# A fused memory attention and two expert layers on one core: attention units seven rounds apart, second-layer weight conversions from block 18 on, three raw buffers, first weights loaded ahead, and the split of g issued later

## The chip, the cores and the metric

The kernel runs as one program on one core of a Trainium2 chip. The metric is the device time of one execution in microseconds (us); the number for the kernel before is the median of three runs.

## The reference

Three stages, all in float32; the weights of the two layers come as float64.

```python
a = softmax(phi, axis=sequence)                     # per batch, head: (576, 32)
k_m, v_m = a.T @ k, a.T @ v                         # (32, 64) each
attn = softmax(q @ k_m.T / sqrt(64), axis=-1) @ v_m
x = attn.transpose(0, 2, 1, 3).reshape(4608, 512)
h = x @ moe_w_in;   g = h - tanh(h);  x = g @ moe_w_out       # d_ff = 2048
h = x @ moe2_w_in;  g = where(h > 0, h, exp(min(h, 0)) - 1);  out = g @ moe2_w_out
```

There are 8 batches, 8 heads, 576 positions and 64 features a head; the layers see 4608 tokens of 512 features.

## The kernel before, in words

Every product is made of three matmuls on split operands: a float32 value is held as a rounded high part and the remainder (low part), and high·high, high·low and low·high are added in PSUM.

**Attention** (`Attention.unit`, lines 108 to 221) works in 16 units of four heads. A unit is a Python generator: each `yield` ends a round, and a unit lasts some 20 rounds. It reduces and exponentiates phi, makes k_m and v_m on TensorE (PE; `km`, line 147), transposes q (`pq`, line 171), forms scores (`sc`, line 192), a softmax over 32 slots, and writes the split probabilities p to memory (line 219). Units 0 and 1 run first; the start rounds of the units are given with `units.at`, for unit 4 and up round 19 and every 6th after.

**First layer** (`Moe1`). The output product of attention is folded into the first weight: `vw_half` (line 293) multiplies v_m by the converted w_in, so h is p times vw (`h_unit`, line 310). The loop over `blocks` (64 of them, index `bi`: two halves of d_ff, four groups of two batches, two sub-sweeps, four blocks of 288 tokens) does in each block two **steps**, i = 0 and 1, for two groups of 256 columns of d_ff. A step issues 12 matmuls of h (line 318), the activation (g_a on ScalarE (ACT), lines 329 to 332; g_b on GpSimd (POOL) and VectorE (DVE), lines 337 and 338; g_c, lines 343 and 344), the split of the g of the step before (g_d: the high part on ACT, line 350, the low part on POOL, line 351), and two x units of 12 matmuls (line 363) that multiply an earlier g by w_out. x units wait in the queue `xq`, so that an x unit uses a g that is about a block old. x goes to memory (line 378), and p of the next block is loaded a block ahead into two buffers (line 290). I number the steps 0 to 127 (step = 2·bi + i); each has one VectorE subtraction of line 338. In the last block of a group the next vw is made in both steps ("vw steps").

**Second layer** (`Moe2`): 18 blocks of 256 tokens, 8 steps each, from about 960 us to the end.

**Conversion of the weights** (`convert`, line 40, driven by `conv`, line 511). One conversion loads 512 KB of float64 words into a raw buffer (line 517 for w_in, 520 for w_out), and builds a float32 value from the two halves of each word: an absolute value into PSUM on ACT (line 48), four passes on DVE (lines 50, 51, 54, 55), the high part on ACT (line 58), the remainder on POOL (line 60). First-layer weights stay in SBUF; second-layer ones are written to memory (line 539) and loaded again in layer two. There are 32 conversions a layer.

What sets the order is a `Staged` queue for the units and one for the conversions (`cv`): a call of `round()` advances every live generator by one stage and starts the next one every `every` rounds. A step calls `cv.round()` once (twice in some blocks) and `units.round()` twice. Where something is not ready, a loop calls rounds on the spot: `need` for a converted weight, the loop on `p_done` for the p of the next block, and `cv.drain()` in `open_l2` at block 60, which opens the buffers of layer two. Each engine executes its instructions in the order in which this program issues them; all loads and stores are issued by SyncE (SP) in that order too.

Of the kernel before, what the change touches and what calls it, by code (L numbers as in the profile page):

```python
# [8 lines left out]
F32 = mybir.dt.float32  # L9
# [9 lines left out]
B, H, S, D, M = 8, 8, 576, 64, 32  # L19
# [16 lines left out]
def r32(ap):  # L36
    return ap.bitcast(F32)
# [25 lines left out]
class Attention:  # L63
# [5 lines left out]
    def __init__(self, tc, ctx, const, ins, vm, p_dram, side, psum):  # L69
        nc = tc.nc  # L70
        self.nc, self.ins, self.vm, self.p_dram = nc, ins, vm, p_dram
        self.ident, self.pmask, self.ones = const["ident"], const["pmask"], const["ones"]
        pool = lambda name, n: ctx.enter_context(
            tc.tile_pool(name=name + side, bufs=n, side=side, reuse_waits="tile"))
        self.wk = pool("at_wk", 1)
        self.sm = pool("at_sm", 3)
        self.sc_p = pool("at_sc", 2 if side == "left" else 1)
        self.ps = psum
        self.q_p = pool("at_q", 2)
        self.loaded = {}  # L80
        fix = pool("at_fix", 1)
        self.kv = fix.tile([128, 2, 4, 6, D], F32, name="kv")
        self.a = fix.tile([128, 6, 4, M], F32, name="a")
        self.kT = fix.tile([128, 4, 2, M], F32, name="kT")
        self.asum = fix.tile([128, 4, M], F32, name="asum")
        for t in (self.a, self.asum, self.kv):
            nc.gpsimd.memset(t[96:], 0.0)
        nc.gpsimd.memset(self.kT, 0.0)
# [19 lines left out]
    def unit(self, u, nxt, eng, first_p=None):  # L108

        nc, wk, sm = self.nc, self.wk, self.sm  # L110
        b, g = divmod(u, 2)
# [3 lines left out]
        ps_tile = lambda shape, name: self.ps.tile(shape, F32, tag="m", name=name)  # L115

        ph = self.loaded.pop((u, "phi"))
        cmax = wk.tile([96, 4, M], F32, tag="cmax", name="cmax")
        nc.vector.tensor_reduce(cmax, ph.rearrange("p h c m -> p h m c"), axis=AX.X, op=ALU.max)
        yield  # L120
        mT = ps_tile([128, 96], "mT")
        nc.tensor.transpose(mT, cmax.rearrange("p h m -> p (h m)"), ident[:96, :96])
        nmax = sm.tile([128, 1], F32, tag="nmax", name="nmax")
        nc.vector.tensor_reduce(nmax, mT, axis=AX.X, op=ALU.max)
        dmax = wk.tile([128, 128], F32, tag="dmax", name="dmax")
        nc.vector.tensor_scalar(dmax, ident, nmax, None, op0=ALU.mult)
        yield
        bmax = ps_tile([96, 4, M], "bmax")
        nc.tensor.matmul(bmax, lhsT=self.ones[:, :96], rhs=dmax, start=True, stop=True)
        bm = wk.tile([96, 4, M], F32, tag="cmax", name="bm")  # L130
        nc.scalar.activation(bm, bmax, ACTF.Copy)
        eng.tensor_tensor(ph, ph, bm.rearrange("p h (o m) -> p h o m", o=1).to_broadcast([96, 4, 6, M]),
                          op=ALU.subtract)
# [344 lines left out]
def moe_kernel(tc, q, k, v, phi, w1, w2, w3, w4, out):  # L478
    nc = tc.nc
    with ExitStack() as top, tc.manual_schedule():  # L480
# [9 lines left out]
        new = lambda stack, name, n, **kw: stack.enter_context(tc.tile_pool(name=name, bufs=n, reuse_waits="tile", **kw))  # L490
        l1a, l1b, l1c, at0_ctx, at1_ctx, wt_ctx, late_ctx, pro, ps_h_ctx = (ExitStack() for _ in range(9))
        m1 = Moe1(tc, l1a, const, p_dram, x2_dram)
        wt_p = {0: new(l1b, "wt0", 1, side="right")}
        vm_p = new(l1b, "vm", 2, side="right")
        cv_p = new(l1b, "cv", 3, side="right")
        raw_p = new(l1b, "raw", 2, side="right")
        wst_p = []
        misc = m1.misc = new(top, "ps_m", 3, space=PSUM)
        cv_ps = new(top, "ps_c", 1, space=PSUM)
# [7 lines left out]
        def need(kind, pg):  # L507
            while not all((1, kind, pg, c) in converted for c in range(2)):
                cv.round()

        def conv(layer, kind, pg, c):

            w = {("i", 1): w1, ("o", 1): w2, ("i", 2): w3, ("o", 2): w4}[kind, layer]
            raw = raw_p.tile([128, 512], mybir.dt.int64, tag="raw", name="raw")
            if kind == "i":
                src = w.rearrange("(k p) f -> p k f", p=128)[:, 2 * c:2 * c + 2, 256 * pg:256 * pg + 256]
                nc.sync.dma_start(out=raw.rearrange("p (a f) -> p a f", a=2), in_=src)
            else:
                r0 = 256 * pg + 128 * c
                nc.sync.dma_start(out=raw, in_=w[r0:r0 + 128, :])  # L520
            yield
            staged = []

            def dst():
                if layer == 1:
                    ws = wi if kind == "i" else wo
                    if c == 0:
                        pool = wt_p[pg // 2 % (2 if kind == "i" else NSW)]
                        shape = [128, 2, 4, 256] if kind == "i" else [128, 2, 2, 512]
                        ws[pg] = pool.tile(shape, F32R, tag=f"w{kind}{pg % 2}", name="w1")  # L530
                    return part(ws[pg], 0, c), part(ws[pg], 1, c)
                staged.append(wst_p[0].tile([128, 2, 512], F32R, tag="wst", name="wst"))
                return staged[-1][:, 0], staged[-1][:, 1]

            yield from convert(nc, cv_p, cv_ps, raw, dst)
            converted.add((layer, kind, pg, c))
            if layer == 2:
                yield
                nc.sync.dma_start(out=w_dram[kind][pg, :, :, 512 * c:512 * c + 512], in_=r32(staged[-1]))

        conv_pair = lambda layer, kind, pg: [conv(layer, kind, pg, c) for c in range(2)]
        conv_l1 = lambda kind, *pgs: [g for pg in pgs for g in conv_pair(1, kind, pg)]
        conv_l2 = [g for pg in range(NPG) for kind in "io" for g in conv_pair(2, kind, pg)]
# [7 lines left out]
        at0.p_done = at1.p_done = p_done = set()  # L551
        new_vm(0)
        nc.vector.memset(r32(vm[0]), 0.0)
        cv = Staged(conv_l1("i", 0, 1) + conv_l1("o", 0, 1), 2)
        for what in "phi", "kv", "q0", "q1":
            at0.load(0, what)
            at1.load(1, what)
        cv.round()

        def unit(u):  # L560
            if u % 4 == 0 and u:
                new_vm(u // 4)
            if u in (0, 2):
                yield from at0.unit(u, 2 if u == 0 else 2 * B, nc.vector if u == 0 else nc.gpsimd,
                                    first_p if u == 0 else None)
            else:
                yield from at1.unit(u, 3 if u == 1 else u + 1, nc.vector if u < 2 else nc.gpsimd,
                                    first_p if u == 1 else None)

        first_p = [m1.new_p(0, n) for n in range(2)]  # L570
        units = Staged()
        for u, t in ((0, 0), (1, 1), (2, 8), (3, 9)):
            units.at(t, unit(u))
        for u in range(4, 2 * B):
            units.at(19 + 6 * (u - 4), unit(u))
        while 1 not in p_done:
            units.round()
            if units.rounds >= 9:
                cv.round()
        pro.close()  # L580
        m1.ps_h = new(ps_h_ctx, "ps_h", 2, space=PSUM)
# [16 lines left out]
        LAG = 4  # L598
        xq, pend, late = deque(), [], []
        at0_open = at1_open = True  # L600

        def x_next(on_act):
            if len(xq) >= LAG:
                sw, n, dm = xq.popleft()
                for i in range(2):
                    need("o", 2 * sw + i)
                m1.x_unit(sw, n, dm, wo, on_act)
                if dm % 2 == 1:
                    late.append((sw, n, dm // 2))

        def store_late():
            while late:
                m1.store_x(*late.pop(0))
# [51 lines left out]
        for bi, (ss, bp, sub, j) in enumerate(blocks):  # L665
# [28 lines left out]
            if at1_open and 2 * B - 1 in p_done:  # L694
# [1 line left out]
                at1_open = False  # L696
                wt_p[3], wt_p[2] = new(l1c, "wt3", 1), new(late_ctx, "wt2", 1)
                cv.first.extend(conv_l1("o", 4, 5))
            if bi == 7:
                cv.todo.extend(conv_l2)  # L700
                cv.every = 3
            if bi == 24:
                cv.first.extend(conv_l1("i", 4, 5))
            if bi == 28:
                cv.first.extend(conv_l1("i", 6, 7) + conv_l1("o", 6, 7))
            if bi == 20:
                cv.every = 2
            if ss == 1 and j == 1 and sub == 1 and bp + 1 < B // 2 or bi == 29:
                load_vm((bp + 1) % (B // 2))
            if nxt and nxt not in m1.p:  # L710
# [1 line left out]
            for i in range(2):  # L712
                pg = 2 * sw + i
                m1.h_unit(sw, n, pg)
                m1.g_a(n, pg)
                m1.g_b(n, pg)
                if pend:
                    m1.g_d(*pend.pop())
                store_late()
                if soon:  # L720
                    soon.popleft()()
                x_next(True)
                cv.round()
                units.round()
                if vw_next:
                    vbp, vpg, pars = vw_next
                    need("i", vpg + i)
                    while ss == 0 and not all(u in vm_done for u in range(4 * vbp + 4)):
                        units.round()
                    m1.vw_half(vm[vbp], wi[vpg + i], vpg + i, 0, pars)  # L730
                if soon and bi > 60:
                    soon.popleft()()
                x_next(bi < 22)
                m1.g_c(n, pg)
                if bi < 7 or 28 <= bi < 30:
                    cv.round()
                units.round()
                if vw_next:
                    m1.vw_half(vm[vbp], wi[vpg + i], vpg + i, 1, pars)
                pend.append((n, pg))  # L740
# [6 lines left out]
        LAG = 1  # L747
# [50 lines left out]
```

## Time and profile before

| | |
|---|---|
| median of three runs | 1791.59 us (1788.22 to 1793.15) |
| the profiled execution | 1789.79 us |
| its span | 1787.6 us |
| PE busy in the span | 1613.6 us (90%) |
| DVE, ACT, POOL busy | 1255.0 (70%), 959.1 (54%), 763.8 us (43%) |
| bytes moved | 238.40 MB, 133 GB/s over the span |
| chain that ended last | PE 62%, DVE 13%, DMA 12%, ACT 6% |

The busy shares are means over stages that differ: attention and the first layer run together until about 490 us, the first layer alone until about 960 us, then the second layer. So the profile is read by stages.

### The profile page before, as it was taken

How to read it: one execution, taken by the hardware profiler on the slowest of the kernel's cores; microseconds unless marked ns; L12 is line 12 of the kernel's file. 1: busy time of each engine (PE TensorE's matmuls, PEld its weight loads, DVE VectorE, ACT ScalarE, POOL GpSimd, SP SyncE). 2: the span in 40 equal slices, each digit the busy share in tenths (PEclk: the TensorE clock that was granted, in tenths of full speed). 3: DMA queues.
4: the chain of work that ended last, by engine and by line, in shares of the span. 5: the costliest groups of instructions: out<-in, count | busy, mean ns of one | idle time of the engine just before them, and what ended most of it. 6: DMA issues, size and time to landing. Idle time of an engine off the chain costs nothing.

```text
span 1787.6 us, 30091 instructions
## 1 busy us (share of the span) xinstructions
PE 1613.6 (90%) x11496; PEld 1483.2 (83%) x11496; DVE 1255.0 (70%) x1805; ACT 959.1 (54%) x1713; POOL 763.8 (43%) x539
## 2 busy tenths in 40 slices
PE   4547787888898999898999999999999999999998
PEld 2336777778897999898999999999999999999997
DVE  5859887988788998888875555555555555555554
ACT  2436776777887887787875333333333333333332
POOL 2235655656665665566653222222222222222222
PEclk9758999999999999999999999999999999999999
DMA  9547577675455445555557621111121121211210
GB/s 214 165 118 191 157 204 215 198 224 181 170 167 168 153 168 190 205 198 205 188 189 276 249 61 57 59 59 58 55 62 58 59 59 57 60 57 59 60 36 24
DMA packets 140934, 238.40 MB, mean 133 GB/s; under 512 B 8184, under 2 KB 102392, under 8 KB 138744
## 3 DMA queue, kind: packets, MB, share of 16 engines
q1 hardware_dynamic: 140792, 236.49, 42.5%
q8 instruction: 91, 1.49, 0.4%
q14 instruction: 51, 0.42, 0.1%
HBM read 159.78 MB, written 75.50 MB: 132 GB/s over the span
## 4 chain that ended last, share of the span: by engine, by line
PE 62%; DVE 13%; DMA 12%; ACT 6%; issue 5%; POOL 2%; SPq 1%; DVEq 0%; ACTq 0%; POOLq 0%
PE h_ps L419 23%; PE o_ps L456 22%; PE x_ps L363 9%; PE h_ps L318 5%; DMA p<-p_dram 5%; DMA raw<-in_moe_w_in_dram 2%; DVE s L343 2%; DVE vw L308 2%; DMA q<-in_q_dram 1%; DMA raw<-in_moe_w_out_dram 1%; DVE h_ps L338 1%; DMA x_dram<-x 1%; ACT t L329 1%; PE vw_ps L303 1%; POOL g L351 1%
## 5 line engine op out<-in xcount | busy, mean ns | idle before, releaser
L363 PE MATMUL x_ps<-g,w 128*128 128x288 f32 x3072 | 448.7, 299 | 40.3 <-DVE vw L308 16.7
L363 PEld LDWEIGHTS x_ps<-g,w 128*128 128x128 f32 x3072 | 422.3, 190 | 52.1 <-ACT x L370 14.7
L419 PEld LDWEIGHTS h_ps<-x,wi 128*128 128x128 f32 x3456 | 429.7, 190 | 11.7
L445 POOL TENSOR_TENSOR e<-hm,e 128x512 fp32r<-128x512 f32 x144 | 186.5, 1295 | 587.3 <-ACT e L444 443.3
L419 PE MATMUL h_ps<-x,wi 128*128 128x256 f32 x3456 | 433.2, 281 | 0.0
L456 PE MATMUL o_ps<-wo,e 128*128 128x512 f32 x1728 | 423.8, 394 | 0.7 <-POOL e L445 0.7
L456 PEld LDWEIGHTS o_ps<-wo,e 128*128 128x128 f32 x1728 | 314.8, 188 | 65.0 <-POOL e L445 1.1
L430 ACT ACTIVATE t_ps<-hm 128x512 f32<-128x512 f32 x144 | 86.7, 602 | 514.3 <-DVE hm L429 514.3
L337 POOL TENSOR_TENSOR v<-t,u 128x576 f32<-128x576 f32 x128 | 183.2, 1431 | 269.2 <-ACT u L330 221.6
L318 PE MATMUL h_ps<-p,vw 128*128 128x288 f32 x1536 | 236.6, 304 | 28.4 <-DMA p<-p_dram 25.2
L318 PEld LDWEIGHTS h_ps<-p,vw 128*128 128x128 f32 x1536 | 217.1, 194 | 33.0 <-issue 24.0
L436 DVE SCALAR_TENSOR_TENSOR hm<-hm,t_ps 128x512 f32<-128x512 f32 x144 | 99.0, 688 | 200.6 <-ACT hm L431 200.6
L351 POOL TENSOR_TENSOR g<-s,g 128x576 fp32r<-128x576 f32 x128 | 183.9, 1437 | 77.0 <-ACT g L350 69.5
L429 DVE TENSOR_SCALAR hm<-h_ps 128x512 f32<-128x512 f32 x144 | 99.6, 692 | 139.0 <-PE h_ps L419 139.0
L343 DVE SCALAR_TENSOR_TENSOR s<-s,v 128x576 f32<-128x576 f32 x128 | 156.5, 1223 | 0.8 <-POOL v L337 0.7
L329 ACT ACTIVATE t<-h_ps 128x576 f32<-128x576 f32 x128 | 83.0, 648 | 90.6 <-issue 43.0
L338 DVE TENSOR_TENSOR h_ps<-h_ps,t 128x576 f32<-128x576 f32 x128 | 98.3, 768 | 35.4 <-ACT u L330 34.4
L344 DVE COPY_PREDICATED s<-big,h_ps 128x576 f32<-128x576 uint32 x128 | 106.6, 833 | 11.0
L308 DVE TENSOR_TENSOR vw<-vw_ps,vw 64x512 fp32r<-64x512 f32 x128 | 88.0, 687 | 36.5 <-ACT vw L306 34.4
L332 ACT ACTIVATE big<-u,bias 128x576 f32<-128x576 f32 x128 | 98.1, 767 | 11.4 <-DVE s L344 11.2
L438 DVE TENSOR_TENSOR hm<-hm,h_ps 128x512 f32<-128x512 f32 x144 | 99.0, 687 | 5.0
L437 DVE SCALAR_TENSOR_TENSOR hm<-hm,t_ps 128x512 f32<-128x512 f32 x144 | 99.0, 687 | 5.0
(86 smaller groups left out, 1776.1 us busy)
## 6 DMA issues: line engine op xcount, KB each, us to landing
x_dram<-x SPq DMA_DIRECT2D x128, 288.0 KB
xr<-x_dram SPq DMA_DIRECT2D x72, 512.0 KB
p<-p_dram SPq DMA_DIRECT2D x62, 576.0 KB
raw<-in_moe_w_in_dram SPq DMA_DIRECT2D x32, 512.0 KB
raw<-in_moe_w_out_dram SPq DMA_DIRECT2D x32, 512.0 KB
w_dram<-wst SPq DMA_DIRECT2D x32, 512.0 KB
kv<-in_k_dram SPq DMA_DIRECT2D x16, 576.0 KB
kv<-in_v_dram SPq DMA_DIRECT2D x16, 576.0 KB
```

The costliest lines, as they stand in the source:

```text
L308: nc.vector.tensor_tensor(lo, src, r32(hi), op=ALU.subtract)
L318: nc.tensor.matmul(ps[:, j, :NB], lhsT=vw[a][:, kc, 128 * j:128 * j + 128], rhs=p[:, kc, b, :], start=(k == 0), stop=(k == 5))
L329: nc.scalar.activation(t, w[0], ACTF.Tanh)
L337: nc.gpsimd.tensor_tensor(v, t, u, op=ALU.mult)
L338: nc.vector.tensor_tensor(h, h, t, op=ALU.subtract)
L343: nc.vector.scalar_tensor_tensor(s, s, G_B, v, op0=ALU.add, op1=ALU.mult)
L344: nc.vector.copy_predicated(s, big.bitcast(U32), d)
L351: nc.gpsimd.tensor_tensor(g[:, 1], s, r32(g[:, 0]), op=ALU.subtract)
L363: nc.tensor.matmul(ps, lhsT=wo[pg][:, a, j, 128 * dm:128 * dm + 128], rhs=g[:, b, j, :], start=(k == 0), stop=(k == 11))
L419: nc.tensor.matmul(ps[:, j], lhsT=w3[:, a, kc, 128 * j:128 * j + 128], rhs=x[:, b, kc, :], start=(k == 0), stop=(k == 11))
L445: nc.gpsimd.tensor_tensor(e[:, 1], hm, r32(e[:, 0]), op=ALU.subtract)
L456: nc.tensor.matmul(self.acc[n][tg], lhsT=e[:, a, j, 128 * tg:128 * tg + 128], rhs=w4[:, b, j, :], start=(pg == 0 and j == 0 and i == 0), s ...
```

## The change

- Units 4 to 15 start at round 22 and every 7th after it, in place of 19 and every 6th.
- The first three conversions issue their loads right after those of units 0 and 1, ahead of everything else; the conversions' rounds begin at round 7 of the units in place of 9.
- A conversion has three raw buffers in place of two, and waits three rounds in place of one between its load and its first instruction (`lead`). To make room the buffer `cv_a` goes from three copies to two, the small attention tiles from three to two, and `dmax` shares the buffer of `cmax`.
- The 32 second-layer conversions enter the queue at block 18 in place of 7, and one starts every second round throughout (before: every third round between blocks 7 and 20).
- g_d is issued behind the x unit and the rounds of its step; an x unit whose g is not split yet is skipped at that point.

```diff
-        self.sm = pool("at_sm", 3)
+        self.sm = pool("at_sm", 2)
...
-        dmax = wk.tile([128, 128], F32, tag="dmax", name="dmax")
+        dmax = row("dmax").rearrange("p h m -> p (h m)")
...
-        cv_p = new(l1b, "cv", 3, side="right")
-        raw_p = new(l1b, "raw", 2, side="right")
+        cv_p = new(l1b, "cv", 2, side="right")
+        raw_p = new(l1b, "raw", 3, side="right")
...
-        def conv(layer, kind, pg, c):
+        def conv(layer, kind, pg, c, lead=2):
...
-            yield
+            for _ in range(lead + 1):
+                yield
...
-        cv = Staged(conv_l1("i", 0, 1) + conv_l1("o", 0, 1), 2)
         for what in "phi", "kv", "q0", "q1":
             at0.load(0, what)
             at1.load(1, what)
-        cv.round()
+        cv_first = [conv(1, "i", k // 2, k % 2, 0) for k in range(3)]
+        cv = Staged([conv(1, "i", 1, 1)] + conv_l1("o", 0, 1), 2)
+        cv.wait = 4
+        for k, g in enumerate(cv_first):
+            next(g)
+            cv.at(2 * k, g)
...
-            units.at(19 + 6 * (u - 4), unit(u))
+            units.at(22 + 7 * (u - 4), unit(u))
         while 1 not in p_done:
             units.round()
-            if units.rounds >= 9:
+            if units.rounds >= 7:
                 cv.round()
...
-            if len(xq) >= LAG:
+            if len(xq) >= LAG and (xq[0][1], 2 * xq[0][0] + 1) in m1.g:
...
-            if bi == 7:
+            if bi == 18:
                 cv.todo.extend(conv_l2)
-                cv.every = 3
...
-            if bi == 20:
-                cv.every = 2
...
                 m1.g_b(n, pg)
-                if pend:
-                    m1.g_d(*pend.pop())
                 store_late()
...
                 x_next(True)
                 cv.round()
                 units.round()
+                if pend:
+                    m1.g_d(*pend.pop())
```

The tables of rounds move instructions on every engine. Three places matter below; lines of the changed kernel are one to six higher than those of the kernel before.

The first is SP's queue at the start, where `raw` is the raw weight of a conversion, `phi`, `kv` and `q` the inputs of an attention unit. Before, and then now:

```order
L105 DMA q<-in_q_dram 96x2x384 x4
L517 DMA raw<-in_moe_w_in_dram 128x2x256
L102 DMA phi<-in_phi_dram 96x4x192 x2
L98 DMA kv<-in_k_dram 96x4x384
L99 DMA kv<-in_v_dram 96x4x384
L98 DMA kv<-in_k_dram 96x4x384
L99 DMA kv<-in_v_dram 96x4x384
L105 DMA q<-in_q_dram 96x2x384 x2
L517 DMA raw<-in_moe_w_in_dram 128x2x256
```

```order
L105 DMA q<-in_q_dram 96x2x384 x4
L518 DMA raw<-in_moe_w_in_dram 128x2x256 x3
L102 DMA phi<-in_phi_dram 96x4x192 x2
L98 DMA kv<-in_k_dram 96x4x384
L99 DMA kv<-in_v_dram 96x4x384
L98 DMA kv<-in_k_dram 96x4x384
L99 DMA kv<-in_v_dram 96x4x384
L105 DMA q<-in_q_dram 96x2x384 x2
L518 DMA raw<-in_moe_w_in_dram 128x2x256
```

Three raw loads in place of one stand ahead of the inputs of units 2 and 3, and the load behind those inputs is the fourth raw load in place of the second.

The second is SP's queue in a block of the second half of d_ff, about 850 us, where `w_dram` takes a converted second-layer weight, `p` is the load for the next block and `x_dram` takes x. Before, and then now:

```order
L539 DMA w_dram<-wst 256x1x512
L517 DMA raw<-in_moe_w_in_dram 128x2x256
L290 DMA p<-p_dram 128x1x1152
L378 DMA x_dram<-x 128x2x288 x2
L539 DMA w_dram<-wst 256x1x512
```

```order
L541 DMA w_dram<-wst 256x1x512
L518 DMA raw<-in_moe_w_in_dram 128x2x256
L379 DMA x_dram<-x 128x2x288
L291 DMA p<-p_dram 128x1x1152
L379 DMA x_dram<-x 128x2x288
L541 DMA w_dram<-wst 256x1x512
```

The conversion's two transfers move from the second step of a block to the first, so that a store of x now lies between them and the load of p.

The third is DVE's queue ahead of step 120, the first of block 60, where `cv_m` and `cv_a` belong to a conversion, `s` to g_c and `h_ps` to g_b. Before, and then now:

```order
L343 SCALAR_TENSOR_TENSOR s<-s,v 128x576
L344 COPY_PREDICATED s<-big,h_ps 128x576
L308 TENSOR_TENSOR vw<-vw_ps,vw 64x512 x2
L338 TENSOR_TENSOR h_ps<-h_ps,t 128x2x288
L372 COPY x<-x_ps 128x288
```

```order
L345 COPY_PREDICATED s<-big,h_ps 128x576
L309 TENSOR_TENSOR vw<-vw_ps,vw 64x512 x2
L50 TENSOR_SCALAR cv_m<-cv_m 128x512
L51 TENSOR_SCALAR cv_m<-cv_m 128x512
L54 SCALAR_TENSOR_TENSOR cv_m<-raw,cv_m 128x512
L55 SCALAR_TENSOR_TENSOR cv_a<-raw,cv_m 128x512
...
L339 TENSOR_TENSOR h_ps<-h_ps,t 128x2x288
```

Now 16 rows of conversion (these four, four times) stand between the vw of step 119 and the subtraction of step 120; before there was none. On SP four `w_dram` stores and the last two raw loads now stand there, ahead of the p of block 61.

## Rows read from the trace of the kernel before

**Rows 1.** Engine totals by stretch: start:end, length, busy (instructions), PE clock, DMA share, GB/s.

```profile
0.00:50.00 50.00, 24.89 (x245) 15.87 (x249) 27.73 (x56) 13.45 (x29) 14.54 (x19) 1.00 0.91 207
110.70:136.90 26.20, 12.90 (x96) 10.20 (x96) 10.80 (x15) 9.74 (x17) 6.68 (x5) 0.61 0.42 107
192.00:488.20 296.20, 252.35 (x2205) 229.37 (x2202) 250.09 (x367) 217.29 (x424) 174.32 (x119) 0.98 0.64 195
216.50:238.50 22.00, 19.73 (x192) 17.96 (x190) 18.46 (x27) 15.66 (x32) 13.85 (x9) 1.00 0.74 184
238.50:259.50 21.00, 17.87 (x172) 15.60 (x171) 16.73 (x29) 15.32 (x28) 8.22 (x6) 1.00 0.68 205
259.50:298.10 38.60, 33.62 (x329) 30.45 (x327) 36.27 (x51) 30.07 (x62) 26.29 (x18) 1.00 0.73 210
298.10:332.10 34.00, 24.22 (x165) 20.96 (x166) 25.18 (x41) 21.12 (x42) 14.27 (x11) 0.90 0.58 180
508.80:526.80 18.00, 18.00 (x138) 17.98 (x137) 17.45 (x26) 16.05 (x28) 14.01 (x10) 1.00 0.60 198
676.00:915.00 239.00, 219.38 (x1622) 214.94 (x1622) 203.87 (x287) 193.93 (x335) 150.23 (x105) 1.00 0.56 194
```

**Rows 2.** DMA issues of the whole run: transfer, issuing queue, count, KB each.

```profile
raw<-in_moe_w_in_dram SPq DMA_DIRECT2D x32, 512.0 KB
kv<-in_k_dram SPq DMA_DIRECT2D x16, 576.0 KB
q<-in_q_dram SPq DMA_DIRECT2D x32, 288.0 KB
phi<-in_phi_dram SPq DMA_DIRECT2D x16, 288.0 KB
```

**Rows 3.** Timeline, 40 to 130 us: start, length, engine, instruction, [idle before it <- releaser].

```profile
42.25 0.70 DVE L50 TENSOR_SCALAR cv_m<-cv_m 128x512 f32<-128x512 f32 x1 [9.82 <-ACT cv_m L48]
126.25 0.70 DVE L50 TENSOR_SCALAR cv_m<-cv_m 128x512 f32<-128x512 f32 x1 [13.49 <-ACT cv_m L48]
```

**Rows 4.** Chain that ended last, to 305 us: start, length, piece.

```profile
26.20 15.31 DMA raw<-in_moe_w_in_dram
...
113.47 12.10 DMA raw<-in_moe_w_in_dram
...
288.13 16.51 DMA raw<-in_moe_w_out_dram
```

**Rows 5.** Groups by line, 676 to 915 us: instruction, count, busy, mean ns, idle before.

```profile
L60 POOL TENSOR_TENSOR wst<-cv_a,wst 128x512 fp32r<-128x512 f32 x21 | 32.5, 1545 | 0.0
L55 DVE SCALAR_TENSOR_TENSOR cv_a<-raw,cv_m 128x512 uint32<-128x512 uint32 x20 | 13.7, 687 | 0.7
L58 ACT ACTIVATE wst<-cv_a 128x512 fp32r<-128x512 f32 x20 | 12.4, 620 | 0.0
L48 ACT ACTIVATE cv_m<-raw 128x512 f32<-128x512 f32 x19 | 12.2, 640 | 8.0 <-DVE cv_a L55 8.0
```

**Rows 6.** Waits: ACT in 298 to 332 us, PE and SP in 676 to 915 us, PE whole.

```profile
ACT cv_m L48 <- DMA raw<-in_moe_w_out_dram: 6.4, 1, 6.4
...
PE h_ps L318 <- DMA p<-p_dram: 10.2, 9, 2.4
...
SPq L539 <- POOL wst L60: 47.9, 21, 2.6
...
PE x_ps L363 <- ACT x L370: 12.7, 10, 1.6
```

**Rows 7.** Timeline around block 60, columns as in rows 3.

```profile
911.78 0.53 SPq L290 DMA_DIRECT2D p<-p_dram  x1
...
920.90 0.77 DVE L338 TENSOR_TENSOR h_ps<-h_ps,t 128x576 f32<-128x576 f32 x1
...
926.72 1.77 PE L318 MATMUL h_ps<-p,vw 128*128 128x288 f32 x12
...
960.17 3.03 PE L419 MATMUL h_ps<-x,wi 128*128 128x256 f32 x24
```

More of the change, by code (lines that the diff above doesn't have):

```diff
@@ L117, in unit @@
         ph = self.loaded.pop((u, "phi"))
-        cmax = wk.tile([96, 4, M], F32, tag="cmax", name="cmax")
+        row = lambda name: wk.tile([128, 4, M], F32, tag="cmax", name=name)
+        cmax = row("cmax")[:96]
         nc.vector.tensor_reduce(cmax, ph.rearrange("p h c m -> p h m c"), axis=AX.X, op=ALU.max)
@@ L129, in unit @@
         nc.tensor.matmul(bmax, lhsT=self.ones[:, :96], rhs=dmax, start=True, stop=True)
-        bm = wk.tile([96, 4, M], F32, tag="cmax", name="bm")
+        bm = row("bm")[:96]
         nc.scalar.activation(bm, bmax, ACTF.Copy)
```

## The prediction

> **What bounds the kernel now.** I read the stages first, then the waits, then the timeline where a wait is long. The stages differ. Between 508.8 and 526.8 us, with no attention left and one conversion under way, TensorE is busy all 18.00 us of four steps: 4.5 us a step is the floor of the first layer [rows 1]. Beside attention a step costs more: 22.0 us for three steps without a conversion (7.33 each), 38.6 us for five with one (7.72), 21.0 us for two vw steps [rows 1]. There PE idles some, and DVE is busy 94% of the stretch with conversions and 84% without [rows 1]. From 192 to 488 us, PE's matmuls leave 296.2 - 252.4 = 44 us idle [rows 1]. Two stretches stand out. At the start the second conversion's absolute value is late and DVE stands 9.82 us, then 13.49 us in step 2 [rows 3]; both times what ended the chain's gap was a raw weight, 15.31 and 12.10 us from issue to landing [rows 4]. And 298 to 332 us takes 34.0 us for three steps, two of them vw steps, where 21.0 + 7.3 would do; a raw load of 16.51 us held ACT for 6.4 us there, and the granted clock averages 0.90, so part of it ran at 1.2 GHz [rows 1, 4, 6]. The second layer, whose first matmul comes at 960.17 us [rows 7], keeps its instructions; the change can only move its beginning.
>
> **The change part by part.**
>
> *Start, to step 0: -5 us.* The transfers are the limit: 0 to 50 us runs at 207 GB/s with a DMA share of 0.91 [rows 1]. Before, up to the second raw weight SP has asked for 4 phi, 8 k or v, 6 q and 2 raw loads, 8,512 KB or 8.72 MB; at 207 GB/s that is 42.1 us, and it did land at 41.5 [rows 1, 2, 4]. Now three raw loads stand in front, and the fourth comes behind the same inputs: 9,536 KB, 9.76 MB, 47 us. So the hole does not close, it moves: DVE waits for conversion four near 48 us, but has then done two conversions more and three rounds of attention more, where the old kernel did these rounds from 42 to 49 us. What is left is one conversion done inside the wait (four passes of 0.69 us, 2.8 us [rows 5]) and unit 4 starting later. Ends: 0 and the whole 9.8 us hole.
>
> *Steps 2 and 3: -16 us.* 110.7 to 136.9 us holds one step of 26.2 us with PE busy 12.9 [rows 1]. The old order forces three rounds of conversion there, for the weight of the first x unit, and with them the absolute value of a weight whose load was issued in that very step. Now that weight is finished, the new load is issued at the same place, but its first instruction stands a step and a half later: 15 us against 12.1. The step should cost like the other vw steps, 10.5 us: -15.7. Ends: 0, if another wait fills the place, and -16. Two small loops (three conversion rounds in steps 6 and 7, about 5 us) and the fewer conversions in steps 3 to 5 cancel.
>
> Here the Trainium skill says otherwise: DMA: Bandwidth & Descriptors, in the section on the anatomy of one DMA, fits a load as 2.0 us plus its bytes at 436 GB/s, which makes 3.2 us of 512 KB (an estimate from that page, and a fit for GpSimd's path). By it no lead could be worth anything here and both these terms would be near 0, the sum 21 us higher; the rows of 12 to 16 us, behind other loads of one queue, speak against it, and I go by the rows.
>
> *Attention, 192 to 488 us: -10 us.* The old kernel runs eight second-layer conversions in steps 17 to 39, the new one none before step 41. Twenty plain steps times 7.72 - 7.33 give -8, the stall at 298 us -6 (34.0 - 28.3) [rows 1]. Given back: a loop of two unit rounds ahead of block 9, where the p of the next batch is not ready (+2), and conversions beside attention in steps 41 to 46 (six times 0.39, +2). The wider spacing by itself I cost at 0: it moves the same PE work from steps 8 to 40 into steps 40 to 46. That holds if PE sets the step. Ends: if a step beside attention costs 7.33 us however few units are in it, seven more such steps cost 7 x 2.83 = +20; if all of PE's idle time goes, -44.
>
> The Trainium skill would see more room: Perfetto Trace Analysis, section "Identifying the Most-Contended Engine", judges TensorE by weight-load busy time and not by matmul time. By it 296.2 - 229.4 = 67 us are idle and not 44, and the lower end of this term would lie 23 us lower; the floor steps, where both read 18.0 of 18.0, cannot tell the two apart.
>
> *Split of g later: -2 us.* ACT now copies x out of PSUM before it copies g, so an x unit of PE that waits for that copy (12.7 us over the run [rows 6]) starts up to 0.6 us sooner, ten times. The g itself is needed a step later, which hides the delay; without that cover each step would pay the copy, 0.6 us. Ends: -12.7 and +2.
>
> *Steps 75 and 76: +9 us.* The longer lead and the later end of attention leave the last two w_out conversions unfinished when the first x unit of the last quarter needs them: four rounds on the spot, eight more DVE passes. PE is in order and stands at that x unit until two pairs of passes (2.8 us, behind 2.2 us of g_b and a pair already there), an absolute value (0.64), the high part (0.62) and the remainder (1.5) are through: 7.7 us [rows 5], and about one more for the clock. Ends: +5 and +12, if the next raw weight is late too.
>
> *p of the next block, 676 to 915 us: -8 us.* PE waits nine times, 10.2 us, for p [rows 6]. SP issues p right behind a weight store and a raw load, and before it stands for the remainder of that weight (47.9 us in 21 waits [rows 6]). Now the pair is issued half a block earlier. Behind it a store of x comes late; three x buffers cover that. Ends: -10.2 and 0.
>
> *Block 60: +16 us.* The conversions that moved back end here: the drain runs 11 rounds at once. DVE has 16 passes in a row (11.1 us), each conversion's absolute value (0.64) between them, as there is one PSUM buffer for it: 13 us [rows 5]. Then follow 0.62 and 1.5 us of the last split, and SP, which stands at the last weight store, issues the p of block 61 some 15.4 us after DVE came to step 120 (920.90), not at 911.78 [rows 7]. With the store ahead of it p takes 1.1 MB at 207 GB/s, 5 us, and lands at 942; step 122 began its h at 926.72 [rows 7]. That is +15, and the idle PE costs a spell at 1.2 GHz, less what later waits absorb: +1. Ends: +10 (PE's two h buffers and p are early) and +24 (the loads of layer two are late as well).
>
> Sum: -5 - 16 - 10 - 2 + 9 - 8 + 16 = **-16 us** on the profiled execution of 1789.8 us, **1774 us**. That execution is 1.8 us below the median of the three runs, so the same cut of the median gives 1776.
>
> **The rivals.**
>
> *A, the late conversions cost more than all gains (slower).* Place: SP at block 60. Behind the last weight store stand not only p but the four x loads of layer two (2.1 MB, 10 us at 207 GB/s) and its first weights (5 us each MB); DVE adds those x in steps 123 and 124 and stands in order for them. If layer two then opens 38 us later instead of 16, and step 75 costs 12: +50 against gains of 41, 1799 us. It decides from 46 us on (41 and the 5.4 us that are 0.3%). For it: nothing of the queue overlaps PE once p is late. Against it: the DMA share before it is 0.56 [rows 1], so there is room to catch up. The Trainium skill has a rule of this kind: Perfetto Trace Analysis, "Optimization Strategy", would have stages with different busiest engines interleaved, and this change takes conversions out of the mix and bunches the last of them; no run here has shown it yet.
>
> *B, the spacing costs.* A step beside attention keeps its 7.33 us because its rounds are a chain across engines: +20, 1794 us. For it: neither PE (90%) nor DVE (84%) is full in those steps [rows 1]. Against it: five steps with conversions were only 0.39 us slower each.
>
> *C, the spacing pays.* With fewer units live, a third of the 44 us of idle time goes: -15 more, 1759 us.
>
> *D, the early loads do not do what they are for.* The second hole only moves one step on, as the raw load behind it is issued where it was, and the first stays: terms one and two are 0, 1795 us.
>
> **How the numbers follow.** The forecast has 0.35, A 0.18, B 0.20, C 0.17, D 0.10. A measurement of this kernel can tell 0.3% (5.4 us) from no change. Faster by more: 0.31 of the forecast, 0.16 of C, 0.06 of B, 0.03 of D, 0.56 in all. Within: 0.03 + 0.01 + 0.02 (A) + 0.10 (B) + 0.04 (D) = 0.20. Slower: 0.01 + 0.16 (A) + 0.04 + 0.03 = 0.24. The range runs from a little below C (1756) to A (1800), and leaves out half of C's and half of A's further side; the forecast's own is 1764 to 1785.
>
> **What would show it.** Right: step 0 near 75 us; no wait over 5 us on a raw weight after that; step 8 at 170 and not 192; the 34 us stretch gone; attention's last unit at step 45; at step 75 a PE wait of 7 us on POOL's remainder; hardly a wait for p between 676 and 900; at block 60 16 DVE passes in a row and PE idle for 10 us or more. Wrong: step 8 still near 190 (D), step 46 later relative to step 8 than the old 296 us (B), or layer two's first matmul more than 20 us further behind the subtraction of step 120 than the 39 us of before (A).

## The result: 1816.6 us, slower

| | before | after |
|---|---|---|
| median, same chip | 1790.99 us (1788.22 to 1793.15) | 1816.60 us (1815.06 to 1821.42) |
| ratio | | 1.0134, 95% interval 1.0112 to 1.0155 |
| profiled execution, its span | 1789.79, 1787.6 us | 1815.06, 1813.3 us |

The forecast was 1774 with a range to 1800. Where the time went shows best by stages. A step starts at its VectorE (DVE) subtraction (line 338, after line 339), as in the prediction. All columns but the first are lengths in us, from one profiled execution each. Kernels e1 to e15 (some numbers are not used) are the experiments below; attention is the column from 8 to 46.

| kernel | step 0 at | 0 to 8 | 8 to 46 | 46 to 75 | 75 to 80 | 80 to 119 | 119 to 124 |
|---|---|---|---|---|---|---|---|
| before | 79.1 | 112.9 | 296.3 | 170.4 | 33.7 | 222.3 | 29.3 |
| after | 75.3 | 95.2 | 299.7 | 180.8 | 41.7 | 220.0 | 55.6 |
| after minus before | -3.8 | -17.7 | +3.4 | +10.4 | +8.0 | -2.3 | +26.3 |
| forecast | -5 | -16 | -12 | 0 | +9 | -8 | +16 |
| e1 split early | 78.0 | 100.2 | 304.9 | 183.6 | 40.8 | 214.6 | 56.7 |
| e2 lead 1 | 76.6 | 94.4 | 303.9 | 176.8 | 40.0 | 214.9 | 52.4 |
| e3 conversions from block 7 | 77.2 | 95.6 | 307.3 | 179.5 | 42.2 | 219.1 | 28.0 |
| e4 p before the drain | 74.8 | 93.8 | 302.6 | 182.1 | 41.7 | 220.3 | 51.1 |
| e5 start 19, every 6th | 76.4 | 108.9 | 280.3 | 178.6 | 32.6 | 221.1 | 63.6 |
| e14 start 22, every 6th | 77.4 | 102.1 | 283.3 | 177.3 | 34.3 | 223.5 | 64.6 |
| e6 head alone | 76.4 | 98.4 | 304.9 | 169.4 | 33.4 | 228.4 | 33.4 |
| e8 small pools alone | 79.2 | 115.3 | 297.9 | 169.5 | 34.8 | 226.1 | 28.1 |
| e15 late split alone | 78.7 | 122.2 | 294.9 | 171.6 | 31.1 | 218.8 | 27.0 |
| e9 combined | 77.5 | 110.8 | 300.2 | 164.7 | 30.7 | 215.1 | 28.0 |
| e12 combined, start 22 | 76.0 | 101.5 | 297.8 | 165.3 | 30.7 | 216.7 | 28.0 |
| e13 e12, split early | 75.8 | 103.4 | 310.4 | 165.2 | 30.2 | 222.1 | 28.4 |

Executions scatter by some 3 us: e4 does what the changed kernel does up to block 60 and differs by 2.9 in attention. Engine totals of the changed kernel, columns as in [rows 1]:

```profile
106.60:117.20 10.60, 7.36 (x43) 6.52 (x41) 5.98 (x8) 5.51 (x10) 4.00 (x3) 0.84 1.06 225
170.50:470.10 299.60, 261.47 (x2286) 240.60 (x2287) 222.50 (x354) 211.29 (x418) 166.27 (x113) 0.97 0.59 173
...
676.00:915.00 239.00, 221.63 (x1625) 218.05 (x1624) 195.99 (x291) 194.74 (x333) 144.26 (x103) 0.99 0.62 197
912.70:955.40 42.70, 20.18 (x112) 19.07 (x111) 23.30 (x34) 16.35 (x28) 14.26 (x11) 0.68 0.54 172
```

Step 2 takes 10.6 us in place of 26.2. In attention DVE has 28 us less to do than in [rows 1] (222.5 against 250.1) and the stretch is no shorter. The last stretch has TensorE (PE) busy 20.2 of 42.7 us. The waits of the changed kernel from 676 to 915 us (total, times, longest), where [rows 6] had 10.2 us for p:

```profile
DVE vw L309 <- ACT vw L307: 23.1, 11, 2.4
ACT cv_m L48 <- DVE cv_a L55: 21.9, 21, 2.5
PE x_ps L364 <- DVE vw L309: 14.4, 11, 2.1
...
PE x_ps L364 <- ACT x L371: 3.0, 6, 0.5
```

The wait for p is gone, as forecast. The first three of these waits were there before, and have grown:

```profile
DVE vw L308 <- ACT vw L306: 12.3, 6, 2.7
PE x_ps L363 <- DVE vw L308: 8.9, 11, 1.0
ACT cv_m L48 <- DVE cv_a L55: 8.0, 11, 1.2
```

What is new lies mostly in the **second vw step** (the second of the two steps that make the next vw), which from block 23 on takes 9.4 us in place of 7.0: all six waits of DVE for ACT's vw lay in first vw steps before, and the five new ones, 2.4 us each, lie in second ones. The timeline of one, step 87, before, columns as in rows 3:

```profile
729.85 0.78 ACT L332 ACTIVATE big<-u,bias 128x576 f32<-128x576 f32 x1 [0.23 <-DVE s L344]
730.54 0.67 ACT L350 ACTIVATE g<-s 128x576 fp32r<-128x576 f32 x1
731.11 0.39 ACT L370 ACTIVATE x<-x_ps 128x288 f32<-128x288 f32 x1
731.40 0.62 ACT L58 ACTIVATE wst<-cv_a 128x512 fp32r<-128x512 f32 x1
731.92 1.18 ACT L306 ACTIVATE vw<-vw_ps 64x512 fp32r<-64x512 f32 x2
```

and after:

```profile
727.78 0.39 ACT L371 ACTIVATE x<-x_ps 128x288 f32<-128x288 f32 x1
...
729.91 0.69 DVE L55 SCALAR_TENSOR_TENSOR cv_a<-raw,cv_m 128x512 uint32<-128x512 uint32 x1
...
730.63 0.63 ACT L48 ACTIVATE cv_m<-raw 128x512 f32<-128x512 f32 x1 [2.46 <-DVE cv_a L55]
731.19 0.67 ACT L351 ACTIVATE g<-s 128x576 fp32r<-128x576 f32 x1
731.76 2.41 ACT L307 ACTIVATE vw<-vw_ps 64x512 fp32r<-64x512 f32 x4
...
732.98 1.39 DVE L309 TENSOR_TENSOR vw<-vw_ps,vw 64x512 fp32r<-64x512 f32 x2 [2.38 <-ACT vw L307]
...
734.51 4.76 PE L364 MATMUL x_ps<-g,w 128*128 128x288 f32 x23 [2.12 <-DVE vw L309]
```

ScalarE (ACT) now meets a conversion's absolute value here. It stands 2.46 us for the one PSUM buffer of `cv_m`, which the conversion before it frees with its last DVE pass; the vw copies stand behind it, DVE behind them, PE behind DVE.

In step 75 the x unit that needs the last first-layer weights waits for their remainders, 4.6 us in all:

```profile
653.99 1.48 PE L364 MATMUL x_ps<-g,w 128*128 128x288 f32 x3 [2.23 <-POOL w L60]
...
657.06 1.49 PE L364 MATMUL x_ps<-g,w 128*128 128x288 f32 x3 [1.59 <-POOL w L60]
...
659.28 0.85 PE L364 MATMUL x_ps<-g,w 128*128 128x288 f32 x2 [0.74 <-POOL w L60]
```

The granted clock of that step is 0.62 on average (engine totals):

```profile
651.00:664.30 13.30, 8.69 (x33) 7.11 (x32) 9.38 (x14) 6.45 (x11) 6.84 (x6) 0.62 0.57 166
```

Block 60, from the first to the last of the 16 passes and on to step 122's h:

```profile
922.05 0.70 DVE L50 TENSOR_SCALAR cv_m<-cv_m 128x512 f32<-128x512 f32 x1
...
927.60 10.90 SPq L541 DMA_DIRECT2D w_dram<-wst  x4
...
935.26 0.69 DVE L55 SCALAR_TENSOR_TENSOR cv_a<-raw,cv_m 128x512 uint32<-128x512 uint32 x1
...
938.59 0.56 SPq L291 DMA_DIRECT2D p<-p_dram  x1
939.04 2.29 PE L364 MATMUL x_ps<-g,w 128*128 128x288 f32 x8 [12.18 <-DVE x L373]
...
950.88 3.22 PE L319 MATMUL h_ps<-p,vw 128*128 128x288 f32 x12 [7.84 <-DMA p<-p_dram]
```

PE idles 12.18 us at an x unit (DVE frees its PSUM buffer behind the passes), then 7.84 us for p, which takes 12.15 us to land.

### The profile page after: what moved, and what is told of

Read it like the earlier page. It is cut to its first block, busy times and chain, and to the rows that moved or that the text cites. A ratio compares the mean times of both kernels' runs of the same rounds, so it can differ in the third digit from the quotient of the medians.

```text
span 1813.3 us, 30112 instructions
## 1 busy us (share of the span) xinstructions
PE 1624.8 (90%) x11496; PEld 1496.5 (83%) x11496; DVE 1215.8 (67%) x1805; ACT 960.8 (53%) x1713; POOL 755.3 (42%) x539
## 4 chain that ended last, share of the span: by engine, by line
PE 68%; DVE 11%; ACT 7%; DMA 7%; issue 4%; POOL 2%; SPq 0%; DVEq 0%; ACTq 0%; POOLq 0%
PE h_ps L420 23%; PE o_ps L457 22%; PE x_ps L364 14%; PE h_ps L319 7%; DMA p<-p_dram 5%; DVE vw L309 2%; ACT vw L307 1%; DVE cv_a L55 1%; DVE cv_m L54 1%; DVE h_ps L339 1%; ACT t L330 1%; PE vw_ps L304 1%; ACT g L351 1%; DVE s L344 1%; ACT u L331 1%
## 5 line engine op out<-in xcount | busy, mean ns | idle before, releaser
L364 PE MATMUL x_ps<-g,w 128*128 128x288 f32 x3072 | 466.2, 305 | 69.0 <-DVE vw L309 27.9
L364 PEld LDWEIGHTS x_ps<-g,w 128*128 128x128 f32 x3072 | 433.6, 195 | 84.5 <-issue 23.9
L319 PE MATMUL h_ps<-p,vw 128*128 128x288 f32 x1536 | 242.5, 310 | 23.8 <-DMA p<-p_dram 21.4
L352 POOL TENSOR_TENSOR g<-s,g 128x576 fp32r<-128x576 f32 x128 | 191.7, 1498 | 146.1 <-ACT g L351 130.7
L319 PEld LDWEIGHTS h_ps<-p,vw 128*128 128x128 f32 x1536 | 223.6, 200 | 27.6 <-issue 15.4
L344 DVE SCALAR_TENSOR_TENSOR s<-s,v 128x576 f32<-128x576 f32 x128 | 114.4, 894 | 4.0 <-POOL v L338 3.9
```

The costliest lines, as they stand in the source:

```text
L319: nc.tensor.matmul(ps[:, j, :NB], lhsT=vw[a][:, kc, 128 * j:128 * j + 128], rhs=p[:, kc, b, :], start=(k == 0), stop=(k == 5))
L344: nc.vector.scalar_tensor_tensor(s, s, G_B, v, op0=ALU.add, op1=ALU.mult)
L352: nc.gpsimd.tensor_tensor(g[:, 1], s, r32(g[:, 0]), op=ALU.subtract)
L364: nc.tensor.matmul(ps, lhsT=wo[pg][:, a, j, 128 * dm:128 * dm + 128], rhs=g[:, b, j, :], start=(k == 0), stop=(k == 11))
```

## The experiments

A ratio is the time over that of the kernel before, run beside it, with its 95% interval. Some expectations name a step by the one that it leads to: their steps 120 and 122 in e3 and e4 are 119 and 121 here, and their vw steps 48 to 112 in e2 are 47 to 111.

**e1 and e2: the split or the conversion?** Both start from the changed kernel.

```diff
# e1
                 m1.g_b(n, pg)
+                if pend:
+                    m1.g_d(*pend.pop())
                 store_late()
...
                 units.round()
-                if pend:
-                    m1.g_d(*pend.pop())
# e2
-        conv_l2 = [g for pg in range(NPG) for kind in "io" for g in conv_pair(2, kind, pg)]
+        conv_l2 = [conv(2, kind, pg, c, 1) for pg in range(NPG) for kind in "io" for c in range(2)]
```

> The changed kernel with the split of g (g_d) back where it was, ahead of the x unit and of the conversion's round; all else as changed. Theory G (the later split is what makes the second step of each vw pair 9.4 us in place of 7.0: the split's high part now stands behind the conversion's absolute value on ACT, and the vw copies behind it): second vw steps after step 46 at 7.6 us or less, nine pairs times 2.3 us = 21 us off, about 1796 us. Rival P (the conversions now have the absolute value in the second step of a block, where the vw copies are, in place of the first; the place of the split does not matter): vw steps stay above 9 us and the time stays within 4 us of 1816.6. If both share it: about 1806.

> The changed kernel with one round less between load and first instruction of the second-layer conversions (lead 1 in place of 2), so that the absolute value, the first DVE passes and the rest fall into the step of a block in which they fell before the change; the split of g stays late. Theory P: second vw steps from step 48 to 112 at 7.6 us or less, about 1796 us. Theory G: they stay above 9 us, within 4 us of 1816.6. The drain has a round less, worth nothing in either.

e1: 1823.0, ratio 1.0154 [1.0115, 1.0194]. e2: 1805.7, ratio 1.0066 [1.0045, 1.0087]. The second vw step is 8.8 us in e1; in e2 it is 9.4 in blocks 27, 31 and 35, where first-layer conversions still have the lead of two, and 7.0 from block 39 on. So in that step the phase (the place of a conversion's instructions in the block) is worth 2.4 us and the split 0.6. Part of the 2.4 comes back in the steps beside it (0.5 in the first vw step, 9.3 against 8.8): over steps 80 to 119, with four pairs, e2 is 5.1 us shorter than the changed kernel, and 7.4 shorter than the kernel before. ACT in e2, in that step:

```profile
728.04 0.39 ACT L371 ACTIVATE x<-x_ps 128x288 f32<-128x288 f32 x1
728.34 0.62 ACT L58 ACTIVATE wst<-cv_a 128x512 fp32r<-128x512 f32 x1
728.86 0.67 ACT L351 ACTIVATE g<-s 128x576 fp32r<-128x576 f32 x1
729.43 1.19 ACT L307 ACTIVATE vw<-vw_ps 64x512 fp32r<-64x512 f32 x2
```

The split is late and the high part of a conversion stands in the queue, but nothing waits. So in the second vw step the phase is the larger cause and the split a small one, but neither theory's numbers were met: 1796 or 1816.6 was expected of e2, and of e1 by P more than 9 us a step and a time within 4 us of 1816.6. And over steps 80 to 119 e1 gains as much as e2 (214.6 and 214.9 us against 220.0), so there the late split and the moved conversions cost together, and taking back either is enough; from 46 to 75 e1 gains nothing. e1 also loses 5 us in the head and 5 in attention.

**e3: conversions as before.**

```diff
-            if bi == 18:
+            if bi == 7:
                 cv.todo.extend(conv_l2)
+                cv.every = 3
+            if bi == 20:
+                cv.every = 2
```

> The changed kernel with the second-layer conversions queued as before (from block 7, every third round, from block 20 every second); units seven rounds apart, early loads and late split stay. Theory drain (the bunched conversions at block 60 cost what the trace shows there, and nothing gives it back): steps 120 and 122 come back from 25.2 and 14.1 to about 6 and 5 us, -28; beside attention eight conversions return, 20 steps times 0.39 = +8, so about 1797 us. Rival (the passes of DVE cost the same wherever they stand, so the drain only shows what is paid elsewhere otherwise): 1810 us or more.

1797.2, ratio 1.0007 [0.9984, 1.0030]: as the theory says. The drain is gone (28.0 us), and attention is 7.6 us longer.

**e4: p ahead of the drain.**

```diff
             if bi == 60:
+                m1.load_p(sw, n + 1)
                 w_first = open_l2()
```

> The changed kernel with the load of p for block 61 issued ahead of the drain at block 60; all else as changed. Theory S (the drain costs twice: the DVE passes ahead of step 120, and SP, which stands for the last weight store before it can issue p): step 120 stays near 25 us, step 122 comes back from 14.1 to about 6, PE's wait of 7.8 us for p there is gone, total 8 to 9 us less, about 1808. Rival (DVE stands at an x that a store still holds, so step 122 stays above 12 us): within 3 us of the changed kernel.

1810.6, ratio 1.0078 [1.0050, 1.0105]. Step 121 falls from 14.1 to 5.0 us, so SP's hold is real; then step 123 grows from 7.7 to 12.2, since the next loads of SP are late in turn (p for PE, x for DVE), and steps 119 to 124 are 4.5 us shorter, not 9. The times are too coarse to tell the two apart (6.0 us between the medians, 0.006 between the ratios). The two waits:

```profile
959.95 3.22 PE L319 MATMUL h_ps<-p,vw 128*128 128x288 f32 x12 [4.48 <-DMA p<-p_dram]
...
961.69 1.22 DVE L402 TENSOR_TENSOR xr<-xr 128x1024 f32<-128x1024 f32 x1 [6.80 <-DMA xr<-x_dram]
```

**e5 and e14: the pitch of the units**, in the changed kernel.

```diff
-            units.at(22 + 7 * (u - 4), unit(u))
+            units.at(19 + 6 * (u - 4), unit(u))       # e5
+            units.at(22 + 6 * (u - 4), unit(u))       # e14
```

> The changed kernel with the units six rounds apart from round 19 again. Theory (the spacing moves work and is worth nothing by itself): steps 8 to 46 take 299.6 us within 4; the wait of step 75 (8.7 us, of which 3.7 come back) is gone as the last first-layer weights are ready sooner; the drain grows by four rounds, two conversions, about +10: within 8 us of the changed kernel's 1.013. Rival B (the spacing costs): steps 8 to 46 at 291 us or less. Rival C (the spacing pays, since the inputs of a unit then have a round more to arrive): 307 us or more.

> The changed kernel with units 4 to 15 six rounds apart from round 22 on: the start as changed, the pitch as before. Theory B (the pitch of seven costs, because a step beside attention takes about as long with fewer units in it, and more steps lie beside it): step 46 at 463 us or earlier in place of 470.1, the wait of step 75 gone (-5 net), the drain four rounds longer (+8): about 1810 us, ratio 1.010 or less. Rival (the pitch is neutral and what e5 showed between steps 8 and 46 only made up for its late start): step 46 within 3 us of 470.1, ratio 1.013 or more.

e5: 1811.6, ratio 1.0100 [1.0066, 1.0134]. e14: 1808.0, ratio 1.0086 [1.0066, 1.0105]. In e14 step 46 starts at 462.8 us against 470.1, and step 75 takes 6.5 us in place of 13.4, so the pitch of seven costs: 7.3 us by step 46, though steps 0 to 8 are 6.9 us longer in e14. That a chain of rounds is the reason, as B has it, is not shown; one place is: step 19 takes 10.8 to 13.2 us in the five kernels with a pitch of seven (the changed one, e1 to e4) and at most 8.2 in all with six. The drain grows by 9. In e5, unit 4 also comes too early for its phi (18.3 us for step 3, where DVE waits 8.2 for it).

**e6 and e8: the head alone, the small pools alone**, in the kernel before. e6 takes these lines of the change with those on `dmax` and `cmax`; e8 takes only the pools, without the line on raw.

```diff
-        self.sm = pool("at_sm", 3)
+        self.sm = pool("at_sm", 2)
...
-        cv_p = new(l1b, "cv", 3, side="right")
-        raw_p = new(l1b, "raw", 2, side="right")
+        cv_p = new(l1b, "cv", 2, side="right")
+        raw_p = new(l1b, "raw", 3, side="right")
...
-        def conv(layer, kind, pg, c):
+        def conv(layer, kind, pg, c, lead=2):
...
+        cv_first = [conv(1, "i", k // 2, k % 2, 0) for k in range(3)]
...
-            if units.rounds >= 9:
+            if units.rounds >= 7:
```

> The kernel before with the head of the change alone: three loads of weights ahead, conversions from round 7 on, lead of two rounds, three raw buffers, the small pools; spacing 6, second-layer conversions from block 7, split of g at its old place. Theory: step 0 near 75 us, step 8 near 171 us, nothing lost later but two rounds of drain at block 60 (0 to 4 us): 1771 us, faster than the kernel before by 18 to 21. Rival (the lead and the two small copies of tiles cost attention what the head gains): step 46 no more than 10 us earlier than before, 1782 us or more.

> The kernel before with the small pools alone (two copies of the small attention tiles and of cv_a, dmax in the buffer of cmax); two raw buffers, no lead, nothing loaded ahead. Theory (the small pools are what ate the head's gain between step 8 and step 46): steps 8 to 46 at 303 us or more in place of 296.2, total up by 6 us or more. Rival (they cost nothing; it is the conversions that the lead shifts behind step 8): steps 8 to 46 within 3 us of 296.2, total within 3 us of before.

e6: 1795.4, ratio 0.9994 [0.9966, 1.0021]. e8: 1796.6, ratio 1.0009 [0.9994, 1.0024]. The head's 17 us at step 8 are there, and lost again, as the rival has it: 8.6 in attention, 6 in steps 80 to 119, 4 in the drain. e8 rules out the pools as the cause in attention (+1.6); in steps 80 to 119 it is itself 3.8 us longer than before, so there they are not ruled out.

**e9, e12, e13: put together.** The changed kernel with

```diff
-        conv_pair = lambda layer, kind, pg: [conv(layer, kind, pg, c) for c in range(2)]
+        conv_pair = lambda layer, kind, pg: [conv(layer, kind, pg, c, 2 if layer == 1 and pg < 4 else 1) for c in range(2)]
...
-            units.at(22 + 7 * (u - 4), unit(u))
+            units.at(19 + 6 * (u - 4), unit(u))       # e9
+            units.at(22 + 6 * (u - 4), unit(u))       # e12, e13
-            if bi == 18:
+            if bi == 11:
```

and in e13 the split early as in e1.

> The changed kernel with units six rounds apart, second-layer conversions from block 11 on and a lead of one round for all conversions but those of the first four column groups, which puts absolute value, DVE passes and remainder into the first step of a block and leaves nothing to drain. Theory P (phase) and drain: from the run with the phase back (1805.7) about 24 us of drain and 5 us of step 75 go, and about 8 us for conversions beside attention come back: 1783 us, ratio 0.993 to before. Rival (what the drain shows is paid elsewhere when it is spread): ratio 1.000 or more.

> The combined kernel with units 4 to 15 started at round 22 in place of 19, still six rounds apart. Theory (the start, not the pitch, is what the change's table gains: with round 19 and the early loads, unit 4 reaches its phi 9.3 us before it has landed, and DVE stands): step 3 to step 8 takes 54 us as in the changed kernel in place of 70.6, half of it stays to step 46 (attention ends a step and a half later), 1764 us, ratio 0.983. Rival (the three rounds come back in full behind step 40, where the last units then run): within 3 us of the combined kernel's ratio 0.986.

> The same, and the split of g back ahead of the x unit. Theory (where the conversions have their old phase, the place of the split is worth nothing in the vw steps, 7.0 us in both; it only decides whether the first x unit waits for its weight in step 2): step 3 some 4 us and step 4 some 6 us later, total up by 3 to 7 us. Rival (the split, if early, leaves 0.6 us in each of 15 vw pairs): total down by 5 us or more.

e9: 1771.7, ratio 0.9864 [0.9828, 0.9900]. **e12: 1761.9, ratio 0.9822 [0.9803, 0.9841]**, faster than both kernels. e13: 1779.4, ratio 0.9927 [0.9907, 0.9946]. In e9 and e12 nothing is left to drain and every second vw step is 7.0 us. e9 was expected at 0.993. It loses 9 us at step 3 to a phi that has not landed, e12 does not (9.9 us against 19.4, though its steps 3 to 8 take 60.9 us, and not the 54 expected). The wait in e9:

```profile
128.92 1.45 DVE L120 TENSOR_REDUCE cmax<-phi 96x128 f32<-96x768 f32 x1 [9.31 <-DMA phi<-in_phi_dram]
```

e13 has the 7.0 us too, so in that step the split's place is worth nothing, as expected; but e13 is 17.5 us slower than e12, far more than either theory gave: 12.6 us in steps 8 to 46, which stay open, and 5.4 in steps 80 to 119, which the waits there account for. First e12, then e13 (SP and PE):

```profile
SPq L541 <- POOL wst L60: 12.0, 20, 0.7
PE h_ps L319 <- DMA p<-p_dram: 1.6, 3, 0.7
```

```profile
SPq L541 <- POOL wst L60: 45.8, 20, 2.6
PE h_ps L319 <- DMA p<-p_dram: 8.0, 7, 2.8
```

With the early split POOL makes the low part of g ahead of a conversion's remainder; SP stands for the remainder with the weight store, and p, behind it in the queue, is late. In steps 80 to 119 SP stands so for 45.8 to 46.5 us in all kernels with the early split (before, e1, e6, e8, e13) and for 9.8 to 12.1 in all with the late one.

**e15: the late split alone**, in the kernel before.

```diff
-            if len(xq) >= LAG:
+            if len(xq) >= LAG and (xq[0][1], 2 * xq[0][0] + 1) in m1.g:
...
-                if pend:
-                    m1.g_d(*pend.pop())
                 store_late()
...
                 units.round()
+                if pend:
+                    m1.g_d(*pend.pop())
```

> The kernel before with the late split of g alone (and the skip of an x unit whose g is not split). Theory (where the conversions keep their phase the late split is worth far more than the 2 us of the prediction, since ACT gives PE its x buffer back before it turns to g): steps 8 to 46 shorter by 5 to 13 us, steps 80 to 119 by 5, ratio 0.989 to 0.995. Rival (the 17 us between the last two runs come from its working together with the early head): ratio 0.998 or more.

1803.3, ratio 1.0055 [1.0036, 1.0075]; its profiled execution, 1794.2, was its fastest. Slower, as the rival's ratio has it; in that one execution 9 us are lost ahead of step 8, attention gains 1.4 and steps 80 to 119 gain 3.5 (PE waits 4.7 us there for p). The late split pays in the combined kernel and not alone; which part of the combination it needs was not found out.

## Why the prediction was wrong

- *Start, steps 2 and 3* (-5, -16): right, -3.8, then -15.6 in step 2 and -1.6 in step 3, and step 8 is at 170.5. By the prediction's estimate from the Trainium skill's fit (DMA: Bandwidth & Descriptors, the anatomy of one DMA; a fit for GpSimd's path) both were to be near 0. The measurement decides for the rows. The hole did not move to conversion four: DVE's L50 waits 0.69 us there at most, and DVE loses 3.78 us to the phi of unit 2 instead.
- *Attention and split* (-12): +3.4. The late conversions gave their -8 (7.6 in e3). "The wider spacing by itself I cost at 0" failed: the pitch costs 7.3 us by step 46 (e14), a third of rival B's price, and the sign named for B came (299.7 us against 296). The split's 2 us can't be told apart in this sum: it is worth 17.5 us in e12 against e13 and costs 0.55% alone (e15). The wait that the term was taken from (12.7 us [rows 6]) did not shrink; in the changed kernel, whole run:

```profile
PE x_ps L364 <- ACT x L371: 13.1, 18, 1.4
```

What the late split does is something that the prediction did not price: it lets SP issue p sooner. And the 34 us stretch was misread. The raw load held ACT, but DVE was held there by a unit's phi (first row: a wait before, 298 to 318 us), and e6 keeps that stretch (13.9 us for step 21) in spite of its lead. Phi is not the whole of it: the late split alone (e15) has 9.8 us there. The changed kernel lost it (7.4) and got another in step 19, of p and a store of x (second and third), which comes with the pitch:

```profile
DVE cmax L119 <- DMA phi<-in_phi_dram: 5.6, 1, 5.6
```

```profile
270.34 3.25 PE L319 MATMUL h_ps<-p,vw 128*128 128x288 f32 x12 [5.18 <-DMA p<-p_dram]
...
271.08 0.41 ACT L371 ACTIVATE x<-x_ps 128x288 f32<-128x288 f32 x1 [7.69 <-DMA x_dram<-x]
```

- *p of the next block* (-8): the waits went, the gain did not. **This is the step that failed most.** "Now the pair is issued half a block earlier" priced the two transfers and nothing else of the moved round. The same shift brings the absolute value into the second vw step, 2.4 us in each of four pairs from step 80 to 119, and with the late split leaves -2.3 of the gain; with the old phase (e2) the stretch has -7.4 and with the old place of the split (e1) -7.7, so the forecast -8 is there as soon as the two do not meet. Four more pairs from step 46 to 75, where I had forecast nothing, with slower steps of two conversion rounds (56 to 58, 22.4 us against 18.1), make +10.4; in e9, with 7.0 us in every second vw step and 16.0 in steps 56 to 58, that stretch is 5.7 us shorter than before. The cause of the gain was also half seen: the earlier pair alone takes the wait for p away (none in e1, where SP still stands 46.5 us for the remainder), but so nearly does the late split alone (1.6 us left in e12).
- *Steps 75 and 76* (+9): right in time, 13.4 us for step 75 against 4.5, and 3.7 come back in step 77; but PE waited 4.6 us for POOL's remainders, not 7.7, and the rest went with matmuls at a clock of 0.62, where about 1 us was set.
- *Block 60* (+16): mechanism right, term mis-sized: +26.3. The passes took 13.9 us (13 forecast), p was issued at 938.59, but landed after 12.15 us, not 5, and in front of the drain stood a slow vw step. e3, which spreads the conversions as before, has 28.0 us in this stretch.

Rival A came true in part: the drain cost 10 us more than forecast, and with the phase it outweighed the head; but A's own sign did not come, as layer two's first matmul was 47.9 us behind the subtraction of step 120, 9 more than before and not 20. C and D fell: the pitch cost, and the early loads did what they were for. The Trainium skill's rule beside A (Perfetto Trace Analysis, "Optimization Strategy") is to interleave stages with different busiest engines. The trace agrees at the drain: spread out again in e3, e9 and e12, the conversions leave 28.0 us of steps 119 to 124 in place of 55.6.

## What to carry over

A round that is moved takes all its instructions along: look at what its first one stands behind on each in-order engine, in every kind of step, not only in the one it was moved for. Work put off past its cover costs a whole burst at the next barrier, and whatever queues behind the barrier's last transfer is late with it. A gain at the head can be lost behind it (e6 lost all of its 17 us, with second vw steps of about 7 us as before), so measure it at the end.

## What was not expected of the hardware

I put a load of p behind one store at 5 us. On the chain of the changed kernel, the loads of p take 12.15 to 16.14 us from issue to landing:

```profile
106.89 15.33 DMA p<-p_dram
...
938.59 12.15 DMA p<-p_dram
959.78 16.14 DMA p<-p_dram
```

The chain of the kernel before could have told it, with seven such loads of 9.56 to 16.12 us:

```profile
660.31 9.56 DMA p<-p_dram
...
934.23 16.12 DMA p<-p_dram
```

And 12 matmuls of h took 3.22 us after the idle time at 950.88 against 1.77 us [rows 7]; the granted clock of that stretch is 0.68 on average, so part of it ran at 1.2 GHz.
